# First stretch of a one-core gated linear attention and MLP kernel: a k product changes engine, keys and values load in another order

## Chip, cores and metric

The kernel runs on one core of one Trainium2 chip. The metric is the device time of one launch in microseconds (us), the median of three runs. Engines are named TensorE (PE, its weight loads PEld), VectorE (DVE), ScalarE (ACT), GpSimd (POOL) and SyncE (SP, which here only issues transfers).

## What is computed

Gated linear attention over 4 batches, 8 heads, 768 steps and 48 channels a head, and then an MLP on its output:

```python
f = 1.0 / (1.0 + np.exp(-f_logit))
for t in range(S):
    state = f[:, :, t, :, None] * state + np.einsum('bhd,bhe->bhde', k[:, :, t], v[:, :, t])
    y[:, :, t] = np.einsum('bhd,bhde->bhe', q[:, :, t], state)
x = attn_out.transpose(0, 2, 1, 3).reshape(B * S, H * D)     # 3072 x 384
h = x @ w_in                                                 # 384 -> 2048
g = h * np.clip(h + 3.0, 0.0, 6.0) / 6.0
out = g @ w_out                                              # 2048 -> 384
```

## The kernel before

**Units.** The sequence of each batch is cut into 6 chunks of 128 steps. A chunk of a batch is a unit: 24 units, those of one chunk over the four batches in a row. Unit i goes through these steps, each a function of `prep` or `core` whose name is the token of the order below (the lines are those of the profile):

- `load` (L408; for unit 0 in two halves, L387) brings the gate logits, `loadq` (L412, L419) queries and keys in one transfer of 512 KB, `loadv` (L423) the values. Unit 0 alone has its keys first by themselves (`loadk`, L412) and then its queries (L419).
- ScalarE makes the sigmoid (`gate`, L390 and L427). VectorE runs a product scan backwards (`back`, L393 and L433) into `suffix`, multiplies the keys by it (`kmul`, L446), makes the reciprocals (`rend`, L451), scans forwards over the same `suffix` tile (`fwd`, L457) and multiplies the queries (`qmul`, L463). So `fwd` of a unit waits until `kmul` of that unit has read `suffix`. `engine("kmul", i)` puts the product on GpSimd if the name stands in the list `ON_POOL`, else on VectorE.
- TensorE transposes the keys (`tk`, L527), ScalarE copies them out (`ktok`, L534), TensorE makes the state's growth (`kv`, L548), ScalarE copies it (`carry0`, L561, and `carry1`, L568). TensorE makes keys by queries (`att`, L508), VectorE masks it (`mask`, L515); TensorE adds queries by state (`qs`, L583) and masked scores by values (`av`, L599). `xh`, `xs`, `xl` (L620, L624, L632) split the result into two halves of 16 bits, and `hole` (L641, two small transfers) fills rows of the MLP's input.

**Weights.** 16 pieces of w_in and w_out: `ld` (L283, 768 KB each) loads one, `cy` and `z` (ScalarE, L296 and L287), `mid`, `dif`, `top` (VectorE, L300, L307, L311), `high` (ScalarE, L316) and `lowi`, `lowo` (L319) turn it into two 16 bit halves.

**MLP.** `mm1a.f` (L844) is the first product for units 0 and 1 with weight piece f, `relua` (L853) and `ga` (L857) the gate, `mm2a` (L862) the second product; `mm1b` and its fellows do units 2 and 3. Later groups use whole or combined blocks (L676, L725, L736, L788).

**Warming matmuls.** `warm.N` multiplies a block of zeros by zeros on TensorE, N times 128 columns, in instructions of at most 512 columns (L1087). Its result is never read. It waits for nothing but the zeros.

**Order.** All instructions of an engine, and all transfers on SyncE's queue, run in the order of one hand-written table, `ORDER`. Each token is issued in turn, and a dependency ties every instruction to the one before it on its engine. `tk.0.3` means step `tk` of unit 0 in PSUM bank 3. Nothing is reordered later, so an instruction that waits holds up all that stands behind it on its engine. SyncE starts a transfer only when the eighth before it has landed.

Of the kernel before, what the change touches and what calls it, by code (L numbers as in the profile page):

```python
# [54 lines left out]
ORDER = """
load.0 loadh.0 gate.0 gateh.0 back.0 backh.0 loadk.0 load.1 loadv.0 loadq.0 rend.0 end.0 kmul.0 fwd.0 gate.1 back.1
warm.16 tk.0.3 ktok.0 warm.4 kv.0.1 carry0.0 load.2 qmul.0 warm.1 att.0.0 loadq.1 ld.0 rend.1 qs.0.2 mask.0 gate.2
end.1 warm.1 av.0 xh.0 kmul.1 tk.1.4 ktok.1 carry1.0 fwd.1 qmul.1 warm.3 att.1.0 xs.0 loadv.1 back.2 mask.1 rend.2 cy.0
load.3 warm.3 kv.1.3 z.0 mid.0 loadq.2 gate.3 end.2 back.3 ld.1 carry0.1 warm.1 qs.1.0 dif.0 kmul.2 top.0 fwd.2 xl.0
carry1.1 loadq.3 av.1 hole.0 tk.2.4 rend.3 xh.1 xs.1 xl.1 z.1 qmul.2 warm.5 att.2.2 kmul.3 cy.1 mid.1 fwd.3 ktok.2  # L60
loadv.2 high.0 warm.4 kv.2.1 carry0.2 end.3 tk.3.4 ktok.3 mask.2 load.4 gate.4 qs.2.0 hole.1 av.2 xh.2 carry1.2 lowi.0
mm1a.0.4 relua.0 dif.1 qmul.3 top.1 high.1 ga.0 loadv.3 xs.2 att.3.2 mask.3 kv.3.1 ld.2 carry0.3 carry1.3 lowi.1 xl.2
loadq.4 warm.1 qs.3.2 av.3 xh.3 mm1a.1.4 cy.2 xs.3 xl.3 relua.1 z.2 back.4 kmul.4 rend.4 fwd.4 ga.1 decay.4 mm2a.0
qmul.4 load.5 gate.5 tk.4.1 mm2a.1 ktok.4 loadv.4 ld.3 cy.3 z.3 hole.2 mid.2 dif.2 top.2 att.4.2 kv.4.3 hole.3 mm1b.0.0
high.2 back.5 mid.3 relub.0 loadq.5 mm1b.1.1 relub.1 lowi.2 gb.0 dif.3 kmul.5 rend.5 gb.1 mm1a.2.4 mm1b.2.0 top.3
mm2b.0 mm2b.1 fwd.5 tk.5.1 relua.2 relub.2 gb.2 qmul.5 ld.4 z.4 cy.4 mid.4 mm2b.2 high.3 ktok.5 lowi.3 ga.2 mm1b.3.0
load.6 gate.6 loadq.6 dif.4 back.6 top.4 load.7 mm1a.3.4 ld.5 relub.3 mm2a.2 relua.3 ga.3 high.4 gb.3 cy.5 z.5 mask.4
mm2a.3 lowi.4 mm1a.4.1 relua.4 rend.6 ld.6 mm1b.4.4 relub.4 loadv.6 gate.7 loadq.7 mm2b.3 carry0.4 kmul.6 fwd.6 mid.5
ga.4 dif.5 z.6 qmul.6 top.5 cy.6 tk.6.1 ktok.6 mm2a.4 back.7 ld.7 decay.5 high.5 qs.4.2 decay.6 att.5.0 gb.4 av.4
kv.6.1 carry1.4 lowi.5 mm1.5.4 mask.5 mm2b.4 carry0.6 xh.4 z.7 xl.4 mid.6 dif.6 kmul.7 carry1.6 loadv.5 kv.5.3 ld.8  # L70
relu.5 g.5 mm2x.5 cy.7 top.6 high.6 cy.8 rend.7 tk.7.0 mid.7 dif.7 load.8 lowi.6 carry0.5 top.7 mm1.6.4 ktok.7 qs.5.2
fwd.7 qmul.7 high.7 loadv.7 relu.6 g.6 z.8 decay.7 att.6.0 ld.9 lowi.7 gate.8 av.5 cy.9 z.9 mask.6 mm1.7.4 relu.7 mid.8
# [96 lines left out]
def gla_moe(ctx: ExitStack, tc: tile.TileContext, fg, qk, v, w, outT):  # L169
# [1085 lines left out]
```

## Time and profile before

| | |
|---|---|
| median of 3 runs | 457.13 us (456.36 to 457.28) |
| profiled execution | 456.43 us, of which the span from the first to the last instruction is 454.7 us |
| TensorE busy | 446.9 us, 98% of the span |
| VectorE, ScalarE, GpSimd busy | 357.5, 232.1, 18.7 us |
| mean granted TensorE clock | 1.00 |
| GpSimd's first k product | 9.80 to 10.98 us |
| first product of the MLP (L844) | from 24.51 us |
| first second product of the MLP (L862) | from 30.08 us |

Times within the profile are us from the span's start. A row of the timeline has start, duration, engine, line, operation, tiles (out<-in, numbers left out), shapes, the count of merged instructions, and in brackets the idle time before and what ended it. TensorE runs a 32 bit matmul in two passes, and each pass is one record: the 16 blocks of `warm.16` are 4 instructions of 512 columns and 8 records. Durations of TensorE are modelled at their end, so the difference of two starts is the safer reading there.

### The profile page before, as it was taken

The page shows a single profiled execution, that of the slowest core. Times are in us where ns is not written, and L with a number is a line of the kernel's source. Part 1 is how long each engine was busy: PE and PEld are TensorE (multiplying, and loading weights), DVE is VectorE, ACT ScalarE, POOL GpSimd, SP SyncE. Part 2 cuts the span into 40 slices and gives each one's busy share as a digit, 9 for nine tenths or more (in the row PEclk, how much of TensorE's full clock was granted, in tenths as well). Part 3 has the DMA queues.
Part 4 walks back from the last instruction along what each step waited for, and adds up shares of the span by engine and source line. Part 5 has one row for each costly group of instructions (what it writes and reads, how often), then busy time and mean ns, then how long its engine had stood idle before and what let it go on. Part 6 is the DMA issues. An engine that isn't in the chain of part 4 may idle for free.

```text
span 454.7 us, 12561 instructions
## 1 busy us (share of the span) xinstructions
PE 446.9 (98%) x5449; PEld 290.4 (64%) x5449; DVE 357.5 (79%) x639; ACT 232.1 (51%) x393; POOL 18.7 (4%) x31
## 2 busy tenths in 40 slices
PE   8899999999999999999999999999999999999996
PEld 5578755544455656676767676666676767677763
DVE  6999999879999999989985855988683677375552
ACT  4786777765454445554554364345253444442431
POOL 3001211231000000000000000000000000000000
PEclk9999999999999999999999999999999999999999
DMA  8769556550242602203202340040000010030002
GB/s 281 252 237 404 201 208 240 200 172 0 62 135 80 180 31 100 69 9 115 91 0 85 99 139 1 25 140 1 2 10 1 7 28 1 1 115 2 1 0 74
DMA packets 25675, 43.18 MB, mean 95 GB/s; under 512 B 2576, under 2 KB 17424, under 8 KB 25616
## 3 DMA queue, kind: packets, MB, share of 16 engines
q1 hardware_dynamic: 24016, 41.56, 27.2%
q8 instruction: 43, 0.70, 0.6%
q10 hardware_dynamic: 1600, 0.79, 0.6%
q14 instruction: 16, 0.13, 0.1%
HBM read 36.43 MB, written 4.72 MB: 91 GB/s over the span
## 4 chain that ended last, share of the span: by engine, by line
PE 95%; DMA 1%; DVE 1%; SPq 1%; ACT 1%; issue 0%; POOL 0%; POOLq 0%
PE o L725 36%; PE pair L788 16%; PE single L788 9%; PE pair L676 7%; PE single L676 5%; PE o L862 3%; PE pair L508 3%; PE pair L599 3%; PE pair L583 3%; PE pair L548 2%; PE o L736 2%; PE pair L527 2%; DMA qkf<-qk 1%; PE o_half L878 1%; PE pair L878 1%; PE single L844 1%
## 5 line engine op out<-in xcount | busy, mean ns | idle before, releaser
L725 PE MATMUL o<-gg,weight 128*128 128x512 f16 x744 | 173.4, 379 | 0.0
L725 PEld LDWEIGHTS <-weight 128*128 128x128 f16 x744 | 71.7, 98 | 73.8
L788 PEld LDWEIGHTS <-weight 128*128 128x128 f16 x672 | 65.0, 98 | 13.2
L788 PE MATMUL pair<-xmem,wide 128*128 128x256 f16 x384 | 51.2, 273 | 0.0
L699 ACT ACTIVATE gg<-raws 128x512 f16<-128x512 f32 x64 | 38.6, 626 | 22.8 <-PE o_half L878 7.2
L788 PE MATMUL single<-xmem,weight 128*128 128x256 f16 x384 | 49.8, 273 | 0.0
L817 ACT ACTIVATE raws<-pair,half 128x512 f32<-128x512 f32 x32 | 21.6, 687 | 42.5 <-PE pair L788 33.6
L788 PEld LDWEIGHTS <-wide 128*128 128x128 f16 x384 | 36.9, 98 | 8.7 <-DVE single L803 0.6
L817 ACT ACTIVATE raws<-single,half 128x512 f32<-128x512 f32 x32 | 22.0, 689 | 38.4 <-PE single L788 37.4
L676 PEld LDWEIGHTS <-weight 128*128 128x128 f16 x243 | 23.1, 98 | 26.7 <-issue 0.3
L788 PE MATMUL pair<-xmem,weight 128*128 128x256 f16 x288 | 36.5, 273 | 0.0
L709 DVE TENSOR_TENSOR gg<-raws,gg 128x512 f16<-128x512 f32 x48 | 31.9, 684 | 5.2 <-ACT gg L699 5.1
L822 DVE SCALAR_TENSOR_TENSOR raws<-raws,single 128x512 f32<-128x512 f32 x32 | 21.8, 683 | 17.5 <-ACT raws L817 17.5
L676 PE MATMUL pair<-xmem,weight 128*128 128x512 f16 x144 | 33.2, 379 | 0.0
L803 DVE TENSOR_TENSOR pair<-pair,raws 128x512 f32<-128x512 f32 x16 | 11.1, 696 | 26.7 <-PE pair L788 23.6
L457 DVE TENSOR_TENSOR_SCAN suffix<-gates,rend 112x516 f32<-112x516 f32 x24 | 29.7, 1237 | 0.8 <-POOL qkf L446 0.7
L822 DVE SCALAR_TENSOR_TENSOR raws<-raws,pair 128x512 f32<-128x512 f32 x32 | 21.5, 681 | 10.6 <-ACT raws L817 10.4
L433 DVE TENSOR_TENSOR_SCAN suffix<-gates,unit 112x516 f32<-112x516 f32 x23 | 28.1, 1224 | 0.0
L676 PE MATMUL single<-xmem,weight 128*128 128x512 f16 x99 | 23.2, 380 | 0.0
L686 ACT ACTIVATE tg<-pair,half 128x512 f32<-128x512 f32 x16 | 10.9, 688 | 19.4 <-PE pair L676 16.2
L699 ACT ACTIVATE gg<-tg 128x512 f16<-128x512 f32 x24 | 14.4, 627 | 8.9 <-DVE tg L690 5.2
L515 DVE TENSOR_TENSOR a<-pair,causal 128x512 f32<-128x512 f32 x24 | 16.3, 683 | 1.9 <-PE pair L548 1.0
(135 smaller groups left out, 637.7 us busy)
## 6 DMA issues: line engine op xcount, KB each, us to landing
raws<-w SPq DMA_DIRECT2D x16, 768.0 KB, 5.9
qkf<-qk SPq DMA_DIRECT2D x23, 512.0 KB, 4.7
gates<-fg SPq DMA_DIRECT2D x23, 258.5 KB, 3.4
v<-v SPq DMA_DIRECT2D x24, 200.0 KB, 3.5
outT<-os SPq DMA_DIRECT2D x11, 256.0 KB, 2.9
outT<-os SPq DMA_DIRECT2D x8, 128.0 KB, 1.9
wide<-wide SPq DMA_DIRECT2D x32, 24.0 KB, 2.1
qkf<-qk SPq DMA_DIRECT2D x2, 256.0 KB, 3.6
```

What stands on the lines that cost most here:

```text
L433: nc.vector.tensor_tensor_scan(flat(sf)[:, ::-1], gt[:, 1:][:, ::-1], flat(unit)[:, ::-1], 0.0, op0=ALU.mult, op1=ALU.add,)
L457: nc.vector.tensor_tensor_scan(flat(sf), gt[:, :NP * (C + 1)], flat(rend), 0.0, op0=ALU.mult, op1=ALU.add,)
L508: nc.tensor.matmul(d["at"][HC * odd:HC * (odd + 1), e, 2 * n + c], t[rs, 1, n, c, odd], t[rs, 0, n, c, odd], start=not growing[at], stop=T ...
L515: nc.vector.tensor_tensor(d["a"].rearrange("r p e t -> r e p t"), d["at"], causal.unsqueeze(1).unsqueeze(1).broadcast_to([128, 2, NP, HC]) ...
L583: nc.tensor.matmul(d["y"][to:to + m, odd, n, cs], before[rs, p, :m], t[rs, 0, n, c, odd], start=alone and (odd, e) not in seen, stop=False ...
L676: nc.tensor.matmul(h, win[:, f, a, k * 128:(k + 1) * 128], g["xt"][:, k, :g["n"] // C, b], start=i == 0, stop=i == 3 * KT - 1,)
L699: nc.scalar.activation(as_t(d, 0), d["t"], AF.Copy)
L709: engine("gl", int(g["name"]) * NF + f).tensor_tensor(as_t(d, 1), d["t"], as_t(d, 0), op=ALU.subtract)
L725: nc.tensor.matmul(g["o"][m], wout[:, f, a, m * 128:(m + 1) * 128], g[f]["gg"][:, b], start=f == 0 and i == 0, stop=f == NF - 1 and i == 2 ...
L788: nc.tensor.matmul(to[:, n * 256:(n + 1) * 256], weights(q, n, a), g["wide"][:, :, block - 3, b], start=fresh and count == 1, stop=count = ...
L817: nc.scalar.activation(to, src, AF.Relu, bias=half, scale=RISE)
L822: nc.vector.scalar_tensor_tensor(to, to, TOP, src, op0=ALU.min, op1=ALU.mult)
```

## The change

The k product of the third unit (`kmul.2`) goes to GpSimd and that of the second (`kmul.1`) to VectorE. The second unit's keys are loaded alone, ahead of its queries, as the first unit's are. The third unit's values (`loadv.2`) are loaded ahead of its queries and keys. The first 230 entries of the order are new; the sum of the warming matmuls stays 39 blocks of 128 columns. Of the order's table two lines stand here:

```diff
 ON_POOL = """
-kmul.1 decay.4 kmul.6 lowi.5 kmul.7 decay.7 lowi.7 kmul.8 gl.9 decay.8 gl.11 qmul.8 gl.12 lowo.0 low.14
+kmul.2 decay.4 kmul.6 lowi.5 kmul.7 decay.7 lowi.7 kmul.8 gl.9 decay.8 gl.11 qmul.8 gl.12 lowo.0 low.14
 """.split()
 ORDER = """
...
+load.0 loadh.0 gate.0 gateh.0 back.0 backh.0 loadk.0 load.1 loadv.0 loadq.0 rend.0 warm.16 kmul.0 warm.4 gate.1 warm.1
+loadk.1 fwd.0 warm.1 warm.3 end.0 back.1 rend.1 loadq.1 tk.0.3 ktok.0 end.1 qmul.0 kmul.1 warm.3 kv.0.1 carry0.0 qs.0.2
...
         def loadq():
-            if i:
+            if i > 1:
                 loadk(slice(0, 2))
             else:
                 nc.sync.dma_start(out=whole[i][:, 0], in_=qk[u][:, 0])
...
         if i == 0:
-            ops.update(halved(sf, gt, rows), loadk=loadk)
+            ops.update(halved(sf, gt, rows))
+        if i < 2:
+            ops["loadk"] = loadk
```

In the changed program all lines behind 474 stand two further down (L527 is L529 there).

TensorE's first rows; `idle` is the target of the warming matmuls, `pair_71` and `pair_70` are PSUM, `qkf_137` is unit 0. Before:

```order
L1087 MATMUL idle<-blank 128x512 x4
L527 MATMUL pair_71<-ident,qkf_137 128x112 x4
L1087 MATMUL idle<-blank 128x512
L548 MATMUL pair_70<-v_140,ktok_157 64x48
L548 MATMUL pair_70<-v_140,ktok_157 48x48
```

And now:

```order
L1089 MATMUL idle<-blank 128x512 x5
L1089 MATMUL idle<-blank 128x128 x2
L1089 MATMUL idle<-blank 128x384
L529 MATMUL pair_71<-ident,qkf_137 128x112 x4
L1089 MATMUL idle<-blank 128x384
L550 MATMUL pair_70<-v_140,ktok_165 64x48
L550 MATMUL pair_70<-v_140,ktok_165 48x48
```

Ahead of the first transposes stood 16 blocks of 128 columns, and now there are 25; between them and `kv.0` stood 4, and now 3.

VectorE between the masks of the second and the third unit; `suffix_81` and `qkf_304` (now `qkf_263`) are unit 2, `suffix_77` and `qkf_326` (now `qkf_318`) unit 3. Before:

```order
L451 RECIPROCAL rend<-suffix_81 112x4
L300 TENSOR_SCALAR raws<-top_274 128x768
L433 SCALAR_TENSOR_TENSOR suffix_77<-gates_76,unit 112x516
L307 TENSOR_TENSOR top_274<-top_274,raws 128x768
L446 TENSOR_TENSOR qkf_304<-qkf_304,suffix_81 112x512
L311 SCALAR_TENSOR_TENSOR wide<-top_274,wide 128x2x384
L457 SCALAR_TENSOR_TENSOR suffix_81<-gates_80,rend 112x516
L451 RECIPROCAL rend<-suffix_77 112x4
L463 TENSOR_TENSOR qkf_304<-qkf_304,suffix_81 112x512
L446 TENSOR_TENSOR qkf_326<-qkf_326,suffix_77 112x512
L300 TENSOR_SCALAR raws<-top_377 128x768
L457 SCALAR_TENSOR_TENSOR suffix_77<-gates_76,rend 112x516
```

And now:

```order
L300 TENSOR_SCALAR raws<-top_284 128x768
L307 TENSOR_TENSOR top_284<-top_284,raws 128x768
L451 RECIPROCAL rend<-suffix_81 112x4
L311 SCALAR_TENSOR_TENSOR wide<-top_284,wide 128x2x384
L433 SCALAR_TENSOR_TENSOR suffix_77<-gates_76,unit 112x516
L457 SCALAR_TENSOR_TENSOR suffix_81<-gates_80,rend 112x516
L446 TENSOR_TENSOR qkf_318<-qkf_318,suffix_77 112x512
L451 RECIPROCAL rend<-suffix_77 112x4
L463 TENSOR_TENSOR qkf_263<-qkf_263,suffix_81 112x512
L457 SCALAR_TENSOR_TENSOR suffix_77<-gates_76,rend 112x516
```

The k product of unit 2 (`qkf_304`) is gone from here, that of unit 3 stands ahead of unit 2's query product instead of behind it, and the second weight piece's `mid` (L300, `top_377`) has moved behind the mask.

ScalarE from the first `relua` on; `middle_106` is `carry0.3`, `state_113` is `carry1.3`, `top_558` (now `top_489`) is `cy.2`, the third weight piece. Before:

```order
L853 ACTIVATE th_0_462<-single,half 128x256
L316 ACTIVATE weight<-wide 128x768
L561 ACTIVATE middle_106<-pair_70 112x2x2x48
L568 ACTIVATE state_113<-pair_70 112x2x2x48
L632 ACTIVATE xmem<-pair_70 112x4x128
L620 ACTIVATE xmem<-pair_71 112x4x128
L296 ACTIVATE top_558<-raws 128x768
```

And now:

```order
L855 ACTIVATE th_0_470<-single,half 128x256
L296 ACTIVATE top_489<-raws 128x768
L563 ACTIVATE middle_106<-pair_70 112x2x2x48
L316 ACTIVATE weight<-wide 128x768
L634 ACTIVATE xmem<-pair_70 112x4x128
L622 ACTIVATE xmem<-pair_71 112x4x128
L454 ACTIVATE ends<-rend 112x4
```

`cy.2`, which reads the third weight piece's transfer, has moved ahead of `carry0.3`.

## Rows read from the trace of the kernel before

**Rows 1.** The page's chain that ended last, shares by engine.
```profile
PE 95%; DMA 1%; DVE 1%; SPq 1%; ACT 1%; issue 0%; POOL 0%; POOLq 0%
```

**Rows 2.** Windows: length, busy us (instructions) by engine, granted clock, DMA share, GB/s.
```profile
17.50:21.00 3.50, 2.70 (x43) 1.75 (x42) 3.37 (x6) 2.98 (x5) 0.00 (x0) 1.00 0.52 157
...
30.00:40.00 10.00, 10.00 (x128) 8.58 (x126) 9.90 (x17) 8.21 (x15) 0.38 (x1) 1.00 0.69 250
```

**Rows 3.** Timeline: GpSimd's first k product.
```profile
9.80 1.18 POOL L446 TENSOR_TENSOR qkf<-qkf,suffix 112x512 f32<-112x512 f32 x1 [6.07 <-DMA qkf<-qk]
```

**Rows 4.** Timeline of VectorE from 9 to 23 us, parts.
```profile
9.60 0.69 DVE L515 TENSOR_TENSOR a<-pair,causal 128x512 f32<-128x512 f32 x1 [0.87 <-PE pair L508]
11.02 1.23 DVE L457 TENSOR_TENSOR_SCAN suffix<-gates,rend 112x516 f32<-112x516 f32 x1 [0.73 <-POOL qkf L446]
...
16.55 0.69 DVE L446 TENSOR_TENSOR qkf<-qkf,suffix 112x512 f32<-112x512 f32 x1
17.15 1.03 DVE L311 SCALAR_TENSOR_TENSOR wide<-top,wide 128x768 int16<-128x768 int16 x1
...
19.48 0.67 DVE L463 TENSOR_TENSOR qkf<-qkf,suffix 112x512 f32<-112x512 f32 x1
20.06 0.68 DVE L446 TENSOR_TENSOR qkf<-qkf,suffix 112x512 f32<-112x512 f32 x1
20.78 0.36 DVE L300 TENSOR_SCALAR raws<-top 128x768 int16<-128x768 int16 x1
...
22.19 0.67 DVE L515 TENSOR_TENSOR a<-pair,causal 128x512 f32<-128x512 f32 x1
```

**Rows 5.** Timeline of TensorE's weight loads, two of the warming matmuls at full pace.
```profile
4.33 0.19 PEld L1087 LDWEIGHTS idle<-blank 128*128 128x128 f32 x1 [0.24 <-issue]
4.76 0.19 PEld L1087 LDWEIGHTS idle<-blank 128*128 128x128 f32 x1 [0.24 <-issue]
```

**Rows 6.** Timeline of TensorE to 31 us, parts.
```profile
6.05 0.55 PE L527 MATMUL pair<-ident,qkf 112*128 112x112 f32 x4
...
7.40 0.91 PE L548 MATMUL pair<-v,ktok 64*64 64x48 f32 x48
...
8.77 0.69 PE L508 MATMUL pair<-qkf 48*64 48x64 f32 x32
9.29 0.41 PE L583 MATMUL pair<-qkf,middle 48*64 48x64 f32 x16
9.63 0.49 PE L1087 MATMUL idle<-blank 128*128 128x128 f32 x2
...
23.89 0.69 PE L599 MATMUL pair<-a,v 64*64 64x64 f32 x32 [0.18 <-DVE top L307]
...
30.08 1.46 PE L862 MATMUL o<-th,wide 128*128 128x256 f32 x6
```

**Rows 7.** Timeline of ScalarE, parts.
```profile
6.64 0.55 ACT L534 ACTIVATE ktok<-pair 128x448 f32<-128x448 f32 x1 [0.40 <-PE pair L527]
8.38 0.33 ACT L561 ACTIVATE middle<-pair 112x192 f32<-112x192 f32 x1 [1.20 <-PE pair L548]
...
27.31 0.33 ACT L561 ACTIVATE middle<-pair 112x192 f32<-112x192 f32 x1 [0.40 <-PE pair L548]
...
29.49 0.90 ACT L296 ACTIVATE top<-raws 128x768 int16<-128x768 int16 x1
```

**Rows 8.** Timeline: a later k product on GpSimd beside a VectorE instruction.
```profile
43.97 1.00 DVE L311 SCALAR_TENSOR_TENSOR wide<-top,wide 128x768 int16<-128x768 int16 x1
44.18 1.79 POOL L446 TENSOR_TENSOR qkf<-qkf,suffix 112x512 f32<-112x512 f32 x1 [13.80 <-DVE suffix L433]
```

**Rows 9.** One line's instructions: forward scans, ns min/median/max, first and last start.
```profile
L457 DVE TENSOR_TENSOR_SCAN suffix<-gates,rend x24: 1212/1227/1490, 5.7 to 332.9; 112x516 f32<-112x516 f32 x24
```

**Rows 10.** The third weight piece's transfer: its issue, and issue to landing.
```profile
21.03 0.43 SPq L283 DMA_DIRECT2D raws<-w  x1
...
DMA to landing us min/median/max: 5.8/5.8/5.8
```

More of the change, by code (lines that the diff above doesn't have):

```diff
@@ L52 @@
 ON_POOL = """
-kmul.1 decay.4 kmul.6 lowi.5 kmul.7 decay.7 lowi.7 kmul.8 gl.9 decay.8 gl.11 qmul.8 gl.12 lowo.0 low.14
+kmul.2 decay.4 kmul.6 lowi.5 kmul.7 decay.7 lowi.7 kmul.8 gl.9 decay.8 gl.11 qmul.8 gl.12 lowo.0 low.14
 """.split()
 ORDER = """
-load.0 loadh.0 gate.0 gateh.0 back.0 backh.0 loadk.0 load.1 loadv.0 loadq.0 rend.0 end.0 kmul.0 fwd.0 gate.1 back.1
-warm.16 tk.0.3 ktok.0 warm.4 kv.0.1 carry0.0 load.2 qmul.0 warm.1 att.0.0 loadq.1 ld.0 rend.1 qs.0.2 mask.0 gate.2
-end.1 warm.1 av.0 xh.0 kmul.1 tk.1.4 ktok.1 carry1.0 fwd.1 qmul.1 warm.3 att.1.0 xs.0 loadv.1 back.2 mask.1 rend.2 cy.0
@@ L59 @@
[L59 to L68, printed above, removed]
@@ L69 @@
-ga.4 dif.5 z.6 qmul.6 top.5 cy.6 tk.6.1 ktok.6 mm2a.4 back.7 ld.7 decay.5 high.5 qs.4.2 decay.6 att.5.0 gb.4 av.4
+load.0 loadh.0 gate.0 gateh.0 back.0 backh.0 loadk.0 load.1 loadv.0 loadq.0 rend.0 warm.16 kmul.0 warm.4 gate.1 warm.1
+loadk.1 fwd.0 warm.1 warm.3 end.0 back.1 rend.1 loadq.1 tk.0.3 ktok.0 end.1 qmul.0 kmul.1 warm.3 kv.0.1 carry0.0 qs.0.2
+load.2 gate.2 ld.0 att.0.0 mask.0 warm.1 fwd.1 qmul.1 tk.1.4 ktok.1 av.0 xh.0 carry1.0 warm.5 xs.0 loadv.1 load.3
+loadv.2 back.2 loadq.2 att.1.0 mask.1 z.0 cy.0 mid.0 dif.0 kv.1.3 carry0.1 carry1.1 rend.2 warm.4 warm.1 top.0 loadq.3
@@ new lines @@
+ld.1 load.4 xl.0 kmul.2 qs.1.0 gate.3 back.3 hole.0 loadv.3 av.1 xh.1 fwd.2 xs.1 xl.1 end.2 tk.2.4 ktok.2 kmul.3 rend.3
+kv.2.1 high.0 qmul.2 carry0.2 cy.1 qs.2.0 fwd.3 att.2.2 mask.2 z.1 mid.1 carry1.2 lowi.0 dif.1 tk.3.4 av.2 ktok.3
+hole.1 mm1a.0.4 xh.2 xs.2 ld.2 qmul.3 gate.4 relua.0 top.1 att.3.2 cy.2 kv.3.1 carry0.3 ga.0 high.1 mask.3 xl.2 qs.3.2
+back.4 av.3 xh.3 loadv.4 lowi.1 mm1a.1.4 loadq.4 kmul.4 end.3 rend.4 decay.4 carry1.3 relua.1 xs.3 mm2a.0 ld.3 xl.3
+tk.4.1 z.2 z.3 ga.1 fwd.4 mid.2 ktok.4 load.5 gate.5 qmul.4 cy.3 dif.2 hole.2 top.2 mm2a.1 high.2 att.4.2 kv.4.3 hole.3
@@ new lines @@
+loadq.5 mm1b.0.0 mm1b.1.1 back.5 mid.3 lowi.2 mm1a.2.4 relub.0 gb.0 relub.1 relua.2 rend.5 kmul.5 fwd.5 mm2b.0 mm1b.2.0
+gb.1 tk.5.1 dif.3 ga.2 mm2b.1 ld.4 z.4 cy.4 mid.4 load.6 gate.6 relub.2 top.3 high.3 qmul.5 loadq.6 gb.2 dif.4 ktok.5
+lowi.3 top.4 back.6 mm2a.2 mm2b.2 high.4 lowi.4 rend.6 mm1b.3.0 mm1a.3.4 relub.3 relua.3 gb.3 ld.5 cy.5 loadq.7 kmul.6
+ld.6 load.7 z.5 mm1a.4.1 relua.4 loadv.6 mask.4 ga.3 fwd.6 mm2b.3 mid.5 ga.4 mm1b.4.4 relub.4 mm2a.3 z.6 gate.7
+carry0.4 dif.5 qmul.6 top.5 cy.6 tk.6.1 ktok.6 mm2a.4 back.7 ld.7 decay.5 high.5 qs.4.2 decay.6 att.5.0 gb.4 av.4
```

## The prediction

> **What bounds the kernel now.** Three views answer this. The chain of waits, summed by engine, shows whether one engine carries the end: TensorE has 95% of it, the rest 1% or less each [rows 1]. The windows show where TensorE is full and where not: from 17.5 to 21 us it is busy 2.70 of 3.50 us, and from 30 to 40 us 10.00 of 10.00, at a granted clock of 1.00 both times, which is the 2.4 GHz level [rows 2]. So behind about 30 us there is no idle time of TensorE to win or to hide in. The change removes no product that is used, and it stands nearly all ahead of that point: whatever delay or gain exists at the first second product of the MLP, at 30.08 us [rows 6], is carried to the end one for one. The question is therefore how the ramp from 4 to 30 us moves. The timelines of TensorE, VectorE and ScalarE over the ramp show that it is a relay: transposed keys, their copy, the state, the mask on VectorE, the scans and products on VectorE, the masks of later units [rows 4, 6, 7]. On VectorE the reader is to see two holes: 0.87 us ahead of the first mask, waiting for TensorE, and 0.73 us ahead of the second unit's forward scan, waiting for GpSimd's k product [rows 4]. The change touches both.
>
> **Step 1, the first transposes.** 25 warming blocks of 128 columns stand ahead of them instead of 16. The pace is read from two weight loads in a row, 4.33 and 4.76 [rows 5]: 0.43 us a record, two records for an instruction of 512 columns, 0.86 us, so 0.215 us a block. Nine blocks more are 9 x 0.215 = 1.93 us, and the transposes move from 6.05 [rows 6] to 7.98. I take this in full, since the matmuls before them wait for nothing. The other end is 0: if the added blocks ran in time in which TensorE now waits for the keys, the transposes would stay. The rows speak for the full price, because at 0.43 us a record TensorE has no gap there to absorb them.
>
> **Step 2, the first mask.** From the transposes on, differences of starts are reused. The keys' copy comes 6.64 - 6.05 = 0.59 later, at 8.57, lasts 0.55 [rows 6, 7] and ends at 9.12; `kv.0`, whose 3 blocks of warming fit in this time, starts at about 9.18. `carry0.0` follows 8.38 - 7.40 = 0.98 later [rows 6, 7], at 10.16, and ends after 0.33 at 10.49. Now `qs.0` stands ahead of `att.0`: 10.55, and it holds TensorE for 9.63 - 9.29 = 0.34 [rows 6], so `att.0` is at 10.89. The mask followed 9.60 - 8.77 = 0.83 later [rows 4, 6]: 11.72, which is 2.12 us late.
>
> **Step 3, the second unit's k product moves to VectorE.** It is one instruction of about 0.68 us, like the other ones there [rows 4]. It stands ahead of the mask, in a hole that was 0.87 us and is now 2.12 us longer, so I cost it at nothing. Its cover goes if its keys land after 11.0 us. GpSimd's product, which waited for keys and queries in one transfer, began at 9.80 [rows 3], and the keys alone are the first half of that, so they are early enough. Behind the mask the forward scan of the second unit follows at the pace of a 0.69 us product, 17.15 - 16.55 = 0.60 [rows 4]: 12.32 against 11.02, 1.30 late. The hole of 0.73 us is gone. **The change wins its 0.73 us here, and has paid 2.12 us for it.**
>
> **Step 4, VectorE to the third unit's query product.** That stretch was 19.48 - 11.02 = 8.46 us, and VectorE is full in it. The third unit's k product leaves it (0.60), the fourth unit's enters (20.78 - 20.06 = 0.72 [rows 4]): 8.58, so 20.90. The second weight piece's first operation leaves a place behind this point, where it costs the mask nothing that I count. Then there is the product on GpSimd beside VectorE. The trace of before has no such pair in the ramp: GpSimd's product took 1.18 us alone [rows 3]. Later, beside a VectorE instruction of two inputs from 43.97 on, one took 1.79 [rows 8], 0.61 more; and of 24 forward scans the slowest took 1490 ns, the median 1227 [rows 9], 0.26 more. The bounds of what VectorE loses are 0 (GpSimd alone is held) and 1.18 (VectorE stands for the whole product). I take 0.60, the middle, near the one price of a collision that I see: 21.5, which is 2.02 late.
>
> The Trainium skill ("SBUF — State Buffer", section "Who interferes with whom") speaks against this step: a VectorE instruction with two inputs in SBUF contends with a GpSimd instruction that reads SBUF, and whoever issues first has the shared ports while the other blocks. That 1.79 stands against 1.18 agrees with it. By it VectorE could lose all of 1.18 us at one product, and the sum would be some 0.6 us higher; that is the second rival.
>
> **Step 5, back on TensorE.** The query product lasts 0.67 and frees `qs.2` at 22.23; with 0.34 for it `att.2` is at 22.57 and the mask at 22.57 + 0.83 = 23.40, against 22.19. It lasts 0.67 [rows 4], and with 0.06 to hand over `av.2` can start at 24.13, against 23.89 [rows 6]. So only 0.24 us of the 1.2 are left: before, `av.2` was released not at the mask's end (22.86) but by a VectorE operation of the weights that stood behind it, `top`, L307 [rows 6]. Of that stretch of 23.89 - 22.86 = 1.03 us the change may keep all or nothing; I take that it goes, since the weight operations now stand ahead of the query product. If it all stayed, the first second product would be about 0.9 us later still, and that end is kept for the range.
>
> **Step 6, ScalarE and the third weight piece.** `cy.2` (0.90 us, at 29.49 before [rows 7]) now stands ahead of `carry0.3`, and reads a transfer that is issued at 21.03 and lands 5.8 us later, at 26.8 [rows 10]. On SyncE's queue it stands behind transfers that have themselves moved: the gates of the fifth unit ahead, the third unit's values ahead of its queries and keys, `hole.0` and `hole.1` behind. So I put its landing at 26.8 to 27.2. Then `cy.2` ends at 27.7 to 28.1, and `carry0.3`, queued behind it, starts 0.4 to 0.8 us after its 27.31 [rows 7]. All that stands behind `carry0.3` on ScalarE, and the state products on TensorE that wait for it, move with it. This contains step 5's 0.24 and isn't added to it. The middle is 0.6 us.
>
> **The sum.** 1.93 in front, 0.19 for the order of `qs.0` and `att.0`, less 0.82 at the scan (its 0.73 us hole and the mask's shorter step), plus 0.12 and 0.60 on VectorE, less 1.78 that the stretch to `av.2` takes up, is 0.24 at 24 us; ScalarE makes it 0.6 at 30.08, so the first second product is at about 30.7. On the profiled execution that is 456.43 + 0.6 = 457.0; that execution has 1.73 us around its span of 454.7 and lies 0.7 below the median, so on the median it is 457.13 + 0.6 = **457.7 us**. A measurement tells about 0.2% from no change, 0.91 us here, so the forecast is no change.
>
> **The rivals.**
> *Slower, by the third weight piece.* One transfer decides: if it lands after about 27.35 us, `cy.2` ends after 28.25 and `carry0.3` is over 0.9 us late. For it speak the regrouped queue and that `cy.2` did not have to hurry before (2.7 us between landing and use); against it, that the transfer needs a delay of over half a microsecond. Price 0.9 to 1.3 us: 458.0 to 458.4. Chance 0.20.
> *Slower, the product on GpSimd does not leave VectorE.* VectorE stands for the whole 1.18 us, so the product has moved in name alone, and 0.6 more comes on top: 458.3. For it speaks [rows 8], against it [rows 9], where the slowest scan lost 0.26 only. Chance 0.10.
> *Slower, by the clock.* The warming blocks are moved to the front, and from 17 to 24 us none is left. There TensorE was busy 2.70 of 3.50 us with them and kept 1.00 [rows 2]; with the work alone it is nearer to half. If the granted clock falls to the 1.2 GHz level for some of this, 3 us of TensorE's work at half speed add 1.5 to 3 us: 458.6 to 460. No row of the ramp shows a fall. Chance 0.08.
> *Faster.* The nine blocks cost nothing, since something else (the keys, say) holds the transposes. Then only the holes of 0.87 and 0.73 us [rows 4] are left, of which the k product fills 0.68, and the whole relay moves ahead by about 1.0: 456.1. The even pace of [rows 5] speaks against it. Chance 0.12.
>
> **How the numbers follow.** No change has 0.50, the three slower rivals 0.20 + 0.10 + 0.08 = 0.38, faster 0.12. The range starts at 456.5, which takes in step 4 at no loss (0.6 less: 457.1) and some of the faster case, and goes to 459.0, which takes in the weight piece, the whole product on VectorE, and the lower part of the clock's price. Outside are most of the faster case and the upper part of the clock's.
>
> **What would show it.** The transposes at about 7.98, the first mask near 11.7, the second unit's scan near 12.3 with no wait for GpSimd, GpSimd's product longer than 1.18 us, the third mask near 23.4, `cy.2` waiting for its transfer near 26.8, the first second product near 30.7 and the clock at 1.00. The argument is wrong if the transposes stay near 6; if delays at 30 us don't reach the end; or if the clock falls between 17 and 24 us.

## The result and the profile after

The changed kernel takes 462.45 us (median of 6 executions, 460.28 to 463.28), the kernel before 456.78 in the same measurement: a ratio of 1.0117 with a 95% interval of 1.0100 to 1.0135. It is slower by some 5.5 us, above the range of the prediction (456.5 to 459.0). The profiled execution has a span of 460.6 us against 454.7.

Each execution comes with its mean granted TensorE clock, and that splits the six: 460.28 and 460.52 us at 1.000 and 0.999, the other four, 462.27 to 463.28, at 0.991 or 0.992. All executions of before in this measurement are between 456.14 and 457.36. So about 3.6 us are lost with the clock at full pace, and some 2.5 more where it falls (462.9, the middle of the four, against 460.4).

The windows of the changed kernel (length, then busy us with instructions for PE, PEld, DVE, ACT, POOL, then granted clock, DMA share, GB/s) answer to [rows 2]:

```profile
17.50:21.00 3.50, 2.84 (x74) 1.90 (x74) 3.10 (x6) 2.06 (x5) 0.00 (x0) 1.00 0.10 31
21.00:24.50 3.50, 2.33 (x54) 1.96 (x54) 3.38 (x5) 2.07 (x6) 0.00 (x0) 0.72 0.29 80
24.50:28.00 3.50, 3.23 (x80) 2.83 (x84) 1.61 (x4) 2.55 (x5) 0.00 (x0) 0.50 0.89 312
28.00:31.50 3.50, 3.49 (x106) 2.70 (x98) 2.81 (x6) 2.41 (x4) 0.00 (x0) 0.80 1.00 381
...
40.00:50.00 10.00, 9.17 (x61) 7.70 (x59) 8.76 (x18) 5.37 (x10) 0.00 (x0) 1.00 1.01 396
50.00:60.00 10.00, 9.49 (x180) 8.04 (x177) 9.66 (x19) 7.01 (x12) 2.11 (x2) 1.00 0.56 202
```

Two things are to be seen. Between 21 and 31 us the clock leaves 1.00 and is at 0.50, the 1.2 GHz level, from 24.5 to 28; from 21 to 24.5 us TensorE was busy only 2.33 of 3.50 us. In finer windows the fall is at about 22.5: from 20.5 to 22.5 TensorE was busy 0.81 of 2.00 us at a clock of 1.00, and from 22.5 to 24.5 the clock is 0.52. And TensorE, which the prediction took as full from 30 us on, is idle 0.83 us between 40 and 50 and 0.51 between 50 and 60.

TensorE's timeline of the same execution answers to [rows 6]:

```profile
8.77 0.55 PE L529 MATMUL pair<-ident,qkf 112*128 112x112 f32 x4
...
17.43 0.55 PE L550 MATMUL pair<-v,ktok 64*48 64x48 f32 x22 [1.01 <-issue]
...
22.79 1.52 PE L550 MATMUL pair<-v,ktok 64*64 64x48 f32 x48 [0.83 <-ACT ktok L536]
24.77 0.70 PE L585 MATMUL pair<-qkf,middle 48*64 48x64 f32 x16 [0.46 <-ACT middle L563]
25.24 1.08 PE L510 MATMUL pair<-qkf 48*64 48x64 f32 x32
...
34.39 1.46 PE L864 MATMUL o<-th,wide 128*128 128x256 f32 x6
```

The first transposes are at 8.77 instead of 6.05, and the first second product of the MLP (L864) at 34.39 instead of 30.08: 4.31 us of the 5.9 by which the spans differ. The products from 22.79 on take longer (1.52 for a `kv` that took 0.91): that is the lower clock.

### The profile page after: what moved, and what is told of

It reads as the page before. It is cut to its first block, busy times and chain, and to the rows that moved or that the text cites. A ratio compares the mean times of both kernels' runs of the same rounds, so it can differ in the third digit from the quotient of the medians.

```text
span 460.6 us, 12562 instructions
## 1 busy us (share of the span) xinstructions
PE 449.4 (98%) x5445; PEld 292.9 (64%) x5449; DVE 358.7 (78%) x639; ACT 231.4 (50%) x393; POOL 18.2 (4%) x31
## 4 chain that ended last, share of the span: by engine, by line
PE 94%; DVE 2%; DMA 1%; ACT 1%; issue 1%; DVEq 0%; ACTq 0%
PE o L727 35%; PE pair L790 16%; PE single L790 9%; PE pair L678 7%; PE single L678 5%; PE pair L601 3%; PE pair L510 3%; PE pair L585 3%; PE idle L1089 2%; PE pair L550 2%; PE o L738 2%; PE pair L529 1%; DMA raws<-w 1%; PE o L864 1%; PE o_half L880 1%; PE pair L880 1%
```

## The experiments

All ran on the chip beside the kernel before, which took 456.6 to 456.8 us (median) each time. Ratios are to it, with 95% intervals.

| run | us | ratio | interval |
|---|---|---|---|
| changed kernel | 462.45 | 1.0117 | 1.0100 to 1.0135 |
| a_more | 460.16 | 1.0074 | 1.0058 to 1.0089 |
| a_front16_moved | 457.88 | 1.0026 | 1.0015 to 1.0037 |
| h_tail_before | 456.47 | 0.9993 | 0.9983 to 1.0002 |
| a_front16 | 458.76 | 1.0049 | 1.0030 to 1.0067 |
| b_front25 | 457.95 | 1.0028 | 1.0018 to 1.0039 |
| h_tail_after | 457.22 | 1.0018 | 1.0005 to 1.0031 |
| a_moved_relub | 458.43 | 1.0041 | 1.0028 to 1.0055 |
| a_relub | 461.80 | 1.0125 | 1.0096 to 1.0155 |
| a_moved_dve | 458.07 | 1.0026 | 1.0017 to 1.0036 |
| b_swap | 456.87 | 1.0002 | 0.9992 to 1.0011 |
| h_cy2 | 456.27 | 0.9993 | 0.9984 to 1.0002 |
| h_front12 | 456.11 | 0.9991 | 0.9982 to 1.0000 |
| h_cy2_front12 | 456.25 | 0.9995 | 0.9986 to 1.0004 |
| b_front12 | 456.91 | 1.0004 | 0.9995 to 1.0012 |
| b_keys_front12 | 455.97 | 0.9985 | 0.9976 to 0.9995 |
| b_keys_front12_again | 456.00 | 0.9987 | 0.9978 to 0.9996 |

The first four rows are a ladder that undoes the change in three steps: nine more warming blocks in the thin stretch (2.3 us less), the front shortened by nine blocks (2.3), and the order behind 30 us put back (1.4).

### The front and the clock

**a_front16**: the nine blocks that the change has more in front are left out.

```diff
-load.0 loadh.0 gate.0 gateh.0 back.0 backh.0 loadk.0 load.1 loadv.0 loadq.0 rend.0 warm.16 kmul.0 warm.4 gate.1 warm.1
-loadk.1 fwd.0 warm.1 warm.3 end.0 back.1 rend.1 loadq.1 tk.0.3
+load.0 loadh.0 gate.0 gateh.0 back.0 backh.0 loadk.0 load.1 loadv.0 loadq.0 rend.0 warm.16 kmul.0 gate.1
+loadk.1 fwd.0 end.0 back.1 rend.1 loadq.1 tk.0.3
```

> The changed kernel without the nine warming blocks that it has more ahead of the first transposes (16 there as before, 30 in all; the warming product computes nothing that is used). The theory that these blocks delay the whole relay: transposes near 6.0 us, first mask near 9.7, and where the clock stays at 1.00 the time is 2.7 us under the changed kernel's undisturbed executions (460.4), about 457.7; with fewer warming products the clock may fall in as many executions or more, and such ones stay about 2.3 us higher, near 460. The rival that the order behind the front (engines, loads, TensorE's new order) costs the time: 460 to 462, as the changed kernel.

Measured: 458.76 us, 3.7 under the changed kernel. Four of eight executions, at a clock of 0.998 to 1.000, took 457.42 to 458.51; the other four, at 0.992 or 0.993, 459.01 to 460.35. Both halves of the expectation hold: the front's price is gone, and the fall of the clock is not.

**a_front16_moved**: the nine blocks stand in the thin stretch instead.

```diff
-av.1 xh.1
+av.1 warm.4 xh.1
...
-tk.2.4 ktok.2 kmul.3 rend.3 kv.2.1 high.0
+tk.2.4 warm.4 ktok.2 kmul.3 rend.3 kv.2.1 warm.1 high.0
```

> The same, with the nine blocks put back behind the second unit's products (4 ahead of the second unit's split, 4 behind the third unit's transposes, 1 behind its state product), so 39 in all. The theory of the front plus the clock: transposes near 6.0 us, clock 1.00 in every execution, about 457.7 us. The rival that the order behind the front costs the time: 460 or more, with the clock at 1.00.

Measured: 457.88 us, 11 of 11 executions at 0.999 or 1.000. The same 39 blocks, placed otherwise, are worth 4.6 us.

**a_more**: the changed kernel with its front, and these nine blocks as well (the diff of a_front16_moved).

> The changed kernel with its front as it is and nine blocks more in the thin stretch at 20 to 25 us (48 in all). If the clock's fall is a cost of its own that comes from idle time there: clock 1.00 in every execution and about 460.4 us, 2 under the changed kernel's median. If the added blocks only stand in the way: 463 or more. If the fall is not due to the idle time: still a clock near 0.992 in most executions and about 462.5.

Measured: 460.16 us, all six executions at 0.998 or 1.000. Its windows:

```profile
17.50:21.00 3.50, 3.08 (x75) 2.21 (x76) 3.15 (x5) 1.66 (x5) 0.35 (x1) 1.00 0.07 25
21.00:24.50 3.50, 3.50 (x60) 2.07 (x59) 3.50 (x6) 2.55 (x6) 0.00 (x0) 1.00 0.27 76
...
40.00:50.00 10.00, 9.20 (x61) 7.71 (x60) 8.80 (x15) 5.95 (x11) 0.85 (x1) 1.00 1.01 394
```

From 21 to 24.5 us TensorE is now busy 3.50 of 3.50 and the clock stays at 1.00. So the fall comes from the idle time there, and costs 2.3 us; the front costs another 2.3 (460.16 against 457.88 for the kernel that differs in the front alone). In the two profiles the first transposes are 2.81 us apart (9.21 and 6.40) and the first second products 2.22 (32.72 and 30.50), so the front is paid nearly in full. At 40 to 50 us TensorE still waits 0.80: a third loss.

**b_front25**: the kernel before with nine blocks more in front.

```diff
-tk.0.3 ktok.0
+warm.4 warm.4 warm.1 tk.0.3 ktok.0
```

> The kernel before with nine blocks more ahead of its first transposes (25 there, 48 in all), nothing else changed. The theory of the front: the transposes move from 6.05 to 8 or 8.8 us and the time rises by 1.9 to 2.7 us, to 458.7 to 459.5. The rival that VectorE's idle time behind it takes the delay up: under 457.5.

Measured: 457.95 us, 1.1 over before, about half of what the same blocks cost in the changed order. That is a result between theory and rival. One would explain it by the hole of 0.73 us on VectorE, which the order of before has and the changed order hasn't; the profile doesn't bear this out. In it the transposes are at 9.00, 2.95 us late, and the second unit's scan at 13.16, 2.14 late, so the hole does take up 0.8. But 0.4 of that is lost again, the first second product is at 32.61, 2.53 late, and this execution, one of the three slowest of nine, took 458.57. Why the median pays only half is open.

### The later order

**h_tail_before**: a_front16_moved up to and with `mm2a.0`, and everything behind it in the order of before.

```diff
-mm2a.0 ld.3 xl.3 tk.4.1 z.2 z.3 ga.1 fwd.4 mid.2
+mm2a.0 xl.3 z.2 fwd.4 ga.1 qmul.4 load.5 gate.5 tk.4.1
```

> The changed kernel with nine warming blocks moved from the front to 20 to 25 us, as in the run before this (457.9 us), and behind the first second product of the MLP all remaining steps in the order of the kernel before. That run lost some 0.4 us up to this product and 1.3 more at 40 to 50 us, where TensorE waited for the gate of a product behind the fifth weight piece on ScalarE. The theory that the later order makes the second loss: TensorE full from 32 us on, 456.5 to 457.0 us. The rival that a late weight piece makes it, in whatever order: the wait stays and the time is 457.7 or more.

Measured: 456.47 us, as the kernel before. Its window is full again:

```profile
40.00:50.00 10.00, 10.00 (x67) 8.57 (x67) 9.48 (x21) 7.49 (x13) 1.69 (x1) 1.00 0.87 350
```

The third loss is the changed order behind 30 us, 1.4 us. One of the twelve executions took 462.95 at a clock of 0.974; no trace shows where that fall was, so this ramp isn't shown to be safe from one.

**h_tail_after**: the other way round, the ramp of before (with `loadk.1` ahead of `loadq.1`) and the changed order behind `mm2a.0`.

```diff
-mm2a.0 qmul.4 load.5 gate.5 tk.4.1 mm2a.1 ktok.4
+mm2a.0 loadv.4 ld.3 tk.4.1 z.3 mid.2 ktok.4 load.5
```

> The kernel before up to its first second product of the MLP (with the second unit's keys loaded alone, and the k products on the engines of before), and behind it all remaining steps in the order of the changed kernel. The theory that the later order costs: TensorE waits 0.8 to 1.4 us at 40 to 50 us, 457.6 to 458.2. The rival that the ramp alone costs: 456.8, as the kernel before.

Measured: 457.22 us, 0.6 over before, and less than expected: in its profile TensorE waits 0.28 us at 47.9. In the profiles the same later order costs more behind the changed ramp than behind the old one: from the first second product to TensorE's last products of the MLP (the last row of L878 or L880) it is 418.42 us before, 418.97 here, 418.39 in h_tail_before and 420.24 in a_front16_moved. The times alone don't separate the two costs, since their intervals overlap.

**a_moved_relub**: a_front16_moved with `relub.2` and `gb.2`, the gate that TensorE waited for, back ahead of the fifth weight piece.

```diff
-ld.4 z.4 cy.4 mid.4 load.6 gate.6 relub.2 top.3 high.3 qmul.5 loadq.6 gb.2 dif.4
+relub.2 gb.2 ld.4 z.4 cy.4 mid.4 load.6 gate.6 top.3 high.3 qmul.5 loadq.6 dif.4
```

> The changed kernel with nine warming blocks moved to 20 to 25 us (457.9 us), and the gate of the first product with weight piece 3 for units 2 and 3 (one ScalarE and one VectorE step) back ahead of the fifth weight piece's steps, as in the order before. The theory that these two steps, queued behind a transfer of 768 KB, are the second loss: the waits of 0.7 and 0.5 us at 43 to 49 us go, 456.5 to 456.9 us. The rival that the loss is spread over the whole later order: 457.4 to 457.9.

Measured: 458.43 us; the theory of the single place falls. TensorE's waits in a_front16_moved were

```profile
43.91 1.56 PE L864 MATMUL o<-th,wide 128*128 128x256 f32 x6 [0.68 <-DVE th L859]
48.94 1.56 PE L864 MATMUL o<-th,wide 128*128 128x256 f32 x6 [0.51 <-DVE th L859]
```

and in this run

```profile
47.48 1.16 PE L846 MATMUL pair<-xmem,weight 128*128 128x256 f16 x9 [0.32 <-ACT weight L316]
49.69 1.56 PE L864 MATMUL o<-th,wide 128*128 128x256 f32 x6 [1.05 <-DVE th L859]
```

The wait at 43.9 is gone. Instead of 0.51 us at 48.9 there are now 0.32 at 47.5, for ScalarE's half of a weight piece (L316), and 1.05 at 49.7, again for a gate.

**a_relub**: the same edit (the same diff) in the changed kernel itself.

> The same two steps put back in the changed kernel itself, its front as it is. If the loss is a place of its own: 1.0 to 1.4 us under the changed kernel, 461.0 to 461.5 where the clock falls and about 459 where it doesn't. The rival that the later loss only follows from the late front: no change, 462.4.

Measured: 461.80 us, three executions at a clock of 1.000 with 459.43 to 460.74 and three at 0.988 to 0.991 with 462.87 to 464.25. As an improvement it fails in the same way. Its profiled execution is the most useful one of the study, though: the edit stands behind 40 us, the clock stays at 1.00, and the ramp is the changed kernel's own. It is read below.

### The engines and the weight piece

**a_moved_dve**: a_front16_moved with `kmul.2` on VectorE.

```diff
-kmul.2 decay.4 kmul.6 lowi.5
+decay.4 kmul.6 lowi.5
```

> The changed kernel with nine warming blocks moved to 20 to 25 us (457.9 us before), and the third unit's k product on VectorE instead of GpSimd, at the same place of the order. VectorE gets 0.68 us more and is spared the waits beside GpSimd (0.1 in a scan there). It stands idle about 0.7 us ahead of the fourth unit's backward scan, so the theory that GpSimd brings nothing here expects 457.6 to 458.2. If GpSimd's product took work off the path: 458.4 or more. If it stood in VectorE's way: under 457.4.

Measured: 458.07 against 457.88, the same ratio. That the product is on GpSimd brings nothing in this order.

**b_swap**: the order of before with only the keys alone and the two products exchanged.

```diff
-rend.1 qs.0.2 mask.0
+rend.1 kmul.1 qs.0.2 mask.0
...
-loadq.1 ld.0
+loadk.1 loadq.1 ld.0
```

> The kernel before with only these parts of the change: the second unit's keys loaded alone, its k product on VectorE (ahead of the first mask), the third unit's k product on GpSimd. Warming blocks and all else in the order of before. If the exchange of engines is a gain that the front and the new order hid: the second unit's forward scan near 10.2 us instead of 11.02 and 456.0 to 456.5 us. If what it frees is taken up by waits further on: 456.6 to 457.1. If GpSimd's product holds VectorE: over 457.3.

Measured: 456.87 us, no change. The second unit's scan comes at 10.50 us instead of 11.02, and then this is to be seen on GpSimd, VectorE and TensorE:

```profile
15.36 2.18 POOL L446 TENSOR_TENSOR qkf<-qkf,suffix 112x512 f32<-112x512 f32 x1 [11.63 <-DMA qkf<-qk]
...
16.53 1.91 DVE L311 SCALAR_TENSOR_TENSOR wide<-top,wide 128x768 int16<-128x768 int16 x1
...
17.60 0.60 PE L529 MATMUL single<-ident,qkf 112*128 112x112 f32 x4 [0.49 <-POOL qkf L446]
```

The product takes 2.18 us instead of 1.18 [rows 3] and VectorE's `top` beside it 1.91 instead of 1.03 [rows 4]: what leaves VectorE (0.6 us) comes back as a longer neighbour, and TensorE waits 0.49 for the product.

**h_cy2**: h_tail_before with `cy.2` behind `carry0.3` again, as before.

```diff
-att.3.2 cy.2 kv.3.1 carry0.3 ga.0 high.1 mask.3 xl.2
+att.3.2 kv.3.1 carry0.3 ga.0 high.1 mask.3 xl.2 cy.2
```

> The changed kernel with nine warming blocks moved from the front to 20 to 25 us and the order of before behind the first second product of the MLP (456.5 us), and the third weight piece's first copy on ScalarE back behind the fourth unit's state copy and split. In that run TensorE waited 0.52 us for this state copy. The theory that the weight piece makes the wait: it goes, and the time falls by 0.3 to 0.5 us, to 456.0 to 456.2. The rival that the copy, now later, holds up what stands behind it: no difference or more, 456.5 and up.

Measured: 456.27 against 456.47, the same ratio of 0.9993. TensorE waits 0.52 us for `carry0.3` with and without the edit: this copy waits for its own product, and the weight piece holds up nothing there. It did in a_front16_moved's profile: the piece came at 26.95, and TensorE waited 1.04 us for `carry0.3`.

### A version that beats both

**h_front12**: h_tail_before with 12 blocks in front.

```diff
-warm.16 kmul.0
+warm.12 kmul.0
...
-kv.0.1
+kv.0.1 warm.2
...
-kv.3.1
+kv.3.1 warm.2
```

> The same 456.5 us kernel with 12 warming blocks ahead of the first transposes instead of 16, and the other four ahead of the first and the fourth unit's state products with queries (two each), where TensorE waited 0.50 and 0.52 us. The theory that each block in front is paid in full in this order: 0.86 us less at the blocks' fast pace, up to 1.4 less where the clock rises late, bounded by the first k product on VectorE that ends at 5.7: 455.6 to 456.2 us. The rival that what stands behind the first transposes takes it up (keys of the second unit, VectorE): 456.3 to 456.8.

Measured: 456.11 us. Against h_tail_before that is 0.4 us less by the medians and 0.1 by the ratios (0.9991 and 0.9993), where 0.3 to 0.9 were expected: most of the earlier front is taken up behind it. In the profiles the transposes are 0.59 us earlier (6.41 and 7.00), the first second product 0.06 (30.36 and 30.42).

**h_cy2_front12**: both edits, of h_cy2 and h_front12.

```diff
-warm.16 kmul.0
+warm.12 kmul.0
...
-att.3.2 cy.2 kv.3.1
+att.3.2 kv.3.1 warm.2
```

> Both of these edits. If they add up: 455.2 to 455.9 us, which beats both kernels. If a single wait decides: as the better of the two.

Measured: 456.25 us. The two do not add up.

**b_front12**: the kernel before with 12 blocks in front and the other four further on.

```diff
-warm.16 tk.0.3
+warm.12 tk.0.3
...
-fwd.1 qmul.1
+fwd.1 warm.2 qmul.1
...
-kv.3.1 ld.2
+kv.3.1 warm.2 ld.2
```

> The kernel before with 12 warming blocks in front instead of 16 and the other four at waits further on, nothing else. If the front alone makes the gain of the run that had this and the keys alone (456.0 us): 456.0. If it takes the second unit's k product on VectorE as well, since GpSimd's product waits for keys and queries until 9.8 us: 456.5 to 456.8, as the kernel before.

Measured: 456.91 us, no change: GpSimd's k product sets the second unit's scan there, and an earlier front only makes its hole longer (1.14 us, with the scan at 11.44).

**b_keys_front12**: the same, with the keys loaded alone and `kmul.1` on VectorE as in b_swap, and `kmul.2` left on VectorE.

```diff
-kmul.1 decay.4 kmul.6 lowi.5
+decay.4 kmul.6 lowi.5
...
-loadq.1 ld.0 rend.1 qs.0.2
+loadk.1 loadq.1 ld.0 rend.1 kmul.1 qs.0.2
```

> The kernel before with the second unit's keys loaded alone and its k product on VectorE ahead of the first mask, the third unit's k product on VectorE as before, and 12 warming blocks in front instead of 16 (the other four at waits further on). If the waits of 0.87 and 0.73 us ahead of the second unit's forward scan set the ramp: its scan near 9.8 us and 455.9 to 456.3 us. If the ramp is set further on, by the chain of later masks and ScalarE, as the exchange of engines in the order of before suggests (456.9): 456.5 to 457.0.

Measured: 455.97 us, ratio 0.9985 (0.9976 to 0.9995). Its VectorE, against [rows 4]:

```profile
8.82 0.69 DVE L446 TENSOR_TENSOR qkf<-qkf,suffix 112x512 f32<-112x512 f32 x1
10.03 0.69 DVE L517 TENSOR_TENSOR a<-pair,causal 128x512 f32<-128x512 f32 x1 [0.52 <-PE pair L510]
10.64 1.22 DVE L457 TENSOR_TENSOR_SCAN suffix<-gates,rend 112x516 f32<-112x516 f32 x1
```

The scan starts at 10.64 instead of 11.02, though the front's blocks ended later than in the profile of before. **b_keys_front12_again** is the same kernel a second time.

> The kernel of 455.97 us once more, on this chip: if its gain is real, 0.4 to 0.7 us under the kernel before; if it was the first run's noise, within 0.2.

Measured: 456.00 us, ratio 0.9987 (0.9978 to 0.9996). The gain is real and small, 0.6 us. What makes it is not shown. The lead of the scan is gone at 16.1 us, where VectorE's `top` starts at 16.09 (16.10 before): from 12.1 to 14.9 the chain that ended last runs over ScalarE (keys' copy, two weight operations, a gate) and no longer over the scan. The first second product comes at 30.39 against 30.08, and TensorE's last products of the MLP are no earlier either. Before:

```profile
448.50 1.47 PE L878 MATMUL pair<-gg,weight 128*128 128x256 f16 x12
```

Here:

```profile
448.73 1.47 PE L880 MATMUL pair<-gg,weight 128*128 128x256 f16 x12
```

These are single executions, and that of before, 456.43, lies 0.1 to 0.4 us under the medians of before in these measurements. b_swap (16 blocks in front, the third unit's product on GpSimd) and b_front12 (12 blocks, without the exchange) each show no change. The version with 16 blocks and both products on VectorE was not run, so it isn't shown that the earlier scan and the shorter front need each other.

## Why the prediction was wrong

Its forecast, no change at 457.7 us, missed 4.8 us. Three steps failed: the sentence of its first part that the change stands nearly all ahead of 30 us, so that nothing is lost behind that point (1.4 us were); the weight of 0.08 given to the clock (2.3 us of the median, by falls in four of six executions); and step 5, by which the ramp takes up 1.78 of 2.02 us and the longer front costs next to nothing (2.3 us by the ladder).

The profile of a_relub, with the clock at 1.00, shows the ramp step by step. TensorE:

```profile
8.04 0.55 PE L529 MATMUL pair<-ident,qkf 112*128 112x112 f32 x4
...
10.89 0.68 PE L510 MATMUL pair<-qkf 48*64 48x64 f32 x32
...
16.67 0.55 PE L550 MATMUL pair<-v,ktok 64*48 64x48 f32 x22 [0.98 <-issue]
...
22.03 0.91 PE L550 MATMUL pair<-v,ktok 64*64 64x48 f32 x48 [0.83 <-ACT ktok L536]
23.39 0.46 PE L585 MATMUL pair<-qkf,middle 48*64 48x64 f32 x16 [0.46 <-ACT middle L563]
23.67 0.65 PE L510 MATMUL pair<-qkf 48*64 48x64 f32 x32
...
25.23 0.69 PE L601 MATMUL pair<-a,v 64*64 64x64 f32 x32 [0.38 <-ACT state L570]
...
31.59 1.46 PE L864 MATMUL o<-th,wide 128*128 128x256 f32 x6
```

VectorE, and the k product on GpSimd:

```profile
11.70 0.69 DVE L517 TENSOR_TENSOR a<-pair,causal 128x512 f32<-128x512 f32 x1 [1.99 <-PE pair L510]
12.31 1.22 DVE L457 TENSOR_TENSOR_SCAN suffix<-gates,rend 112x516 f32<-112x516 f32 x1
...
16.00 0.89 DVE L300 TENSOR_SCALAR raws<-top 128x768 int16<-128x768 int16 x1
...
18.87 1.23 DVE L433 TENSOR_TENSOR_SCAN suffix<-gates,unit 112x516 f32<-112x516 f32 x1 [0.33 <-ACT gates L427]
...
21.81 0.66 DVE L463 TENSOR_TENSOR qkf<-qkf,suffix 112x512 f32<-112x512 f32 x1
...
24.39 0.69 DVE L517 TENSOR_TENSOR a<-pair,causal 128x512 f32<-128x512 f32 x1 [0.77 <-PE pair L510]
...
15.49 1.19 POOL L446 TENSOR_TENSOR qkf<-qkf,suffix 112x512 f32<-112x512 f32 x1 [11.76 <-DVE suffix L433]
```

**Steps 1 to 3 came out in this execution.** Transposes at 8.04 (7.98 predicted), `att.0` at 10.89 (10.89), first mask at 11.70 (11.72), second unit's scan at 12.31 (12.32), with no wait for GpSimd. In the changed kernel's own profile all of it stands 0.73 later, because TensorE reached its faster level later (below). So step 1's 1.93 us holds only where that level comes early: with 25 blocks in front the transposes are at 8.04, 8.77 and 9.21 (a_more) in the profiles of the changed order, up to 1.2 us later than predicted.

**Step 4 was right in its term, and left one out.** The query product comes 9.50 us behind the scan, 9.18 were predicted. GpSimd's product lengthened `mid` from 0.36 [rows 4] to 0.89 us: 0.53, where I had put 0.60. The Trainium skill ("SBUF — State Buffer", "Who interferes with whom") says of VectorE's modes that use two ports, which a `tensor_scalar` such as `mid` can enter, that whoever issues first has the ports shared with GpSimd for its whole instruction and the other blocks. The 0.89 agrees: the product had begun at 15.49, ahead of `mid`, and ended at 16.68. In b_swap both engines lost time beside each other. The missing 0.33 us is the wait for a gate on ScalarE. The chain back from it: the gate stands behind `carry0.1`, this waits for `kv.1`, and `kv.1` stops for 0.98 us in its middle.

**Step 5 failed.** It let `att.2` follow the query product, with `qs.2` ahead of it. In the new order `kv.2` stands ahead of both on TensorE: it waits 0.83 us for the keys' copy, and `qs.2` then 0.46 for the state's copy. The query product ended at 22.47, `att.2` began at 23.67 instead of 22.57. The third mask is at 24.39 (23.40 predicted), and `av.2` at 25.23 (24.13). The piece of the order that I showed was VectorE's; what stands ahead of a wait on the waiting engine, TensorE, was not looked through there. That is 1.1 us. The path was wrong from step 3 on: in the chain that ended last of this execution VectorE has, between 10 and 24 us, the first mask alone. Of TensorE's pieces of this chain (start, length, what):

```profile
13.13 1.28 PE idle L1089 x4
...
15.69 0.98 issue
...
17.23 1.28 PE idle L1089 x4
```

Two groups of five warming blocks (`idle`) and the stop inside `kv.1` stand on it, and behind them the split of the second unit and the keys' copy for which `kv.2` waits. No run took these ten blocks away, so what they cost is not shown.

**Step 6 was there, but mis-sized.** ScalarE in the same profile (its first row is the `carry0.1` of step 4):

```profile
17.28 0.33 ACT L563 ACTIVATE middle<-pair 112x192 f32<-112x192 f32 x1 [1.65 <-PE pair L550]
...
28.04 0.90 ACT L296 ACTIVATE top<-raws 128x768 int16<-128x768 int16 x1 [0.52 <-DMA raws<-w]
28.84 0.32 ACT L563 ACTIVATE middle<-pair 112x192 f32<-112x192 f32 x1
```

`cy.2` did wait for its weight piece, which came at 28.0, later than the 27.35 from which the first rival was to decide. But `carry0.3` would not have started much sooner, since its own product ended at 28.52 (27.67 + 0.85), so the price was some 0.3 us on ScalarE and not 0.9; h_cy2 found 0.2 for it, within its noise, and in a_front16_moved TensorE's wait was 0.5 longer than in h_tail_before. The first second product came at 31.59, 1.51 late where 0.6 were predicted.

**The carry to the end.** From 30 us on, a delay is carried one for one: a_more and a_front16_moved differ by 2.22 us there (32.72 and 30.50) and by 2.28 in time, and from the first second product to TensorE's last products of the MLP the profiles with the later order of before have 418.3 to 418.6 us, at first second products between 30.08 and 32.61. But the 230 entries of new order reach past 48 us, and I read no place of them behind 30. [rows 2] says that TensorE was full there in the order of before; it says nothing on a new order: the changed kernel and its variants with the changed later order have 420.0 to 420.5 us for this stretch.

**The clock.** The rival named place and price: idle time from 17 to 24 us without warming blocks, 1.5 to 3 us. Measured were 2.3. Its chance was wrong, and two details: five blocks do stand in that stretch (17.91 to 19.19 in the changed kernel; the clock fell at about 22.5), and the price was put on the time of before, 457.13, and not on the 457.7 of the sum. That the rows of before show no fall was no evidence, since the change takes out the very blocks that stood there.

The rival that GpSimd's product holds VectorE for all of its 1.18 us didn't happen here (0.53), and neither did the one on the other side: in the changed order the front's blocks cost nearly their full time.

**What is open.** Which entries of the later order make the 1.4 us was not found: one place put back only moved the wait. Why the later order costs more behind the changed ramp (1.8 us in the profiles, 1.4 in time) than behind the old one (0.6 in both) was not tried.

## What to carry to other kernels

Warming work has a place, not only a sum: the same 39 blocks cost 4.6 us more at the front, ahead of a chain that sets the end, than in the stretch where TensorE would idle and its clock fall. When an order is made anew, walk the queue of the waiting engine through every wait you price, and walk the new order to its end and not to the point where the old trace was full. A hole on an engine that is closed need not gain anything: here such an exchange and a shorter front showed no change by themselves, and a version of both gained 0.6 us, so try such edits in pairs too, and look at what the chain runs over behind the hole.

## What the runs showed of the hardware

**TensorE's slow start differs between executions.** Weight loads of the warming blocks, in the changed kernel:

```profile
3.85 0.34 PEld L1089 LDWEIGHTS idle<-blank 128*128 128x128 f32 x1 [0.52 <-issue]
4.71 0.34 PEld L1089 LDWEIGHTS idle<-blank 128*128 128x128 f32 x1 [0.52 <-issue]
5.53 0.19 PEld L1089 LDWEIGHTS idle<-blank 128*128 128x128 f32 x1 [0.49 <-issue]
5.96 0.19 PEld L1089 LDWEIGHTS idle<-blank 128*128 128x128 f32 x1 [0.24 <-issue]
```

and in a_relub, which is the same program up to there:

```profile
2.99 0.34 PEld L1089 LDWEIGHTS idle<-blank 128*128 128x128 f32 x1 [0.52 <-issue]
3.85 0.29 PEld L1089 LDWEIGHTS idle<-blank 128*128 128x128 f32 x1 [0.52 <-issue]
4.37 0.19 PEld L1089 LDWEIGHTS idle<-blank 128*128 128x128 f32 x1 [0.24 <-issue]
4.80 0.19 PEld L1089 LDWEIGHTS idle<-blank 128*128 128x128 f32 x1 [0.24 <-issue]
```

The loads are 0.86 us apart at first and 0.43 later, the ratio of the 1.2 and the 2.4 GHz level, while the granted clock of the windows reads 1.00 throughout (0 to 4 and 4 to 10 us). The step came at about 5.5 us in one execution and 4.3 in the other, in the same order of the same instructions, and moved the transposes from 8.77 to 8.04. The Trainium skill ("TensorE: Matmul & The Clock Gate", "Part 1: The HAM clock gate") says that the number of slow matmuls at a kernel's start varies from run to run; these rows agree. With 16 blocks in front the transposes came between 6.05 and 7.51 us in the profiles, so a front that is measured in blocks is not measured in time.

**A fall of the clock is not the same in every execution.** The changed kernel fell in four of six, a_front16 in four of eight, a_relub in three of six, each of them one program in one order.

**TensorE stops inside a group of products with no releaser.** The stop in the middle of `kv.1` ("issue"), 0.79 to 1.50 us long, stands in every run with the changed ramp, and always at one of two places of the group: behind 26 of its 48 products with the long front, behind 34 with 16 blocks or fewer. In h_tail_after, with the ramp of before, there is one of 0.28 us behind 32. The transfers of this stretch hold one packet of instructions, in the changed kernel from 14 to 16 us:

```profile
q1 hardware_dynamic: 182, 0.83, 100.1%
q8 instruction: 1, 0.02, 3.4%
```

In the profiles of the changed kernel, a_relub, a_front16_moved and h_tail_before TensorE goes on 1.3 to 1.5 us behind the end of such a packet. That TensorE waits there for its own instructions, behind a queue that is full of data, fits; it is argued and was not tested, and the kernel before has such a packet too, to 13.3 us, and no stop.
